# Two chunks of tokens at a time through the dense layers, with 512-column products of h

## The chip, the cores and the metric

The kernel runs on one core of one Trainium2 chip. The metric is device time in microseconds (us), the median of several executions. Engines in the rows: PE is TensorE's products, PEld its weight loads, DVE is VectorE, ACT is ScalarE, POOL is GpSimd, SP is SyncE, which issues most DMAs.

## The reference, cut to what matters

Sliding-window attention with sink tokens, then a gated two-layer block on its output:

```python
# q, k, v: (4 batches, 8 heads, 768, 64) float32; window 128, 4 sink tokens
scores = (q @ k.T) / sqrt(64)              # kept: first n_sink columns, and 0 <= row - col < window
a = exp(scores - max); a = a / (a.sum() + 1e-9)
x = (a @ v)                                # heads side by side: 3072 tokens x 512
h = x @ w_in                               # 512 x 2048, float64 in memory
g = h * cos(h)
out = g @ w_out                            # 2048 x 512, float64 in memory; out float32
```

## The kernel before, in words

The 3072 tokens are twelve chunks of 256 (`NT = CB * P`). A chunk is a batch and a first block of 128 rows. The first three chunks are the heads of batches 0 to 2 (row 0 on); then the others follow batch by batch. For each chunk eight attention heads are worked through, and their outputs become x, transposed (512 rows of 256 tokens), split into a rounded high part `xhi` and a remainder `xlo` so that a product in the reduced fp32r format keeps float32's accuracy. The weights are loaded as 64-bit words, converted on VectorE (L540 to L555), and split into `hi` and `lo` too.

The dense layers of a chunk go in eight slots (`NSLOT`) of two 128-row tiles of the hidden dimension (`FG = 2`). In a slot, `h_mm` (L411) makes h for two tiles: per tile 4 blocks of the contraction x 3 products (lo x hi, hi x hi, hi x lo), each with 128 columns of w_in as weights and 256 tokens moving. Then come, on 128 x 512 values each: `turns` (ScalarE, h in turns, rounded to a whole number), `rest` (VectorE, the remainder), `cosine` (ScalarE, sine table), `gate` (VectorE, in place in the h bank), `g_hi` (ScalarE) and `g_lo` (VectorE). `out_mm` (L467) multiplies g by w_out, 512 columns moving, and accumulates over all 16 tiles into two accumulators `acc`, one per 128 tokens. When the eight slots are done, the accumulators are copied (`out_copy`) and stored; those of the last chunk by `last_rows` (L1443), after the check whether a general path is needed. Chunk 0 takes g and w_out unsplit, in full float32 (`x.full`, L474).

PSUM has eight banks: `b0`, `b1` for the accumulators; `b4` and `b2`, and from chunk 2 on `b3` too, for h (L1418); `s` for scores, `tp` for the transposed probabilities, `av` for the attention's values product and for the sinks' transpose `gp`. A bank of h is free when `g_lo` has read it; a bank of scores when the masks have.

The order is written out by a planner, `Plan`. Each step has a priority time, an estimated duration, the engine or engines that may run it, and what it depends on: other steps, or a buffer (`buf(tag, n)`: the step waits for the users of the buffer's previous holder). `Plan.order` plays the steps through: whenever an engine is free, it takes the ready step with the smallest key, which is the priority with penalties for a change of table (`PEN`), for GpSimd or for a second-choice engine. The order so found is emitted, and each engine then runs its list in order, waiting on semaphores. The framework adds the waits, also between engines that touch one PSUM tile. The priority times are the constants `C`: slot s of chunk a stands at `S1 + ((a-1)*NSLOT + s)*T` (chunk 0 at `S0 + s*STEP`), a head at `S1 + (g - 16)*T`, so that the attention of a chunk runs one chunk ahead of its dense slots. Heads of the first 24 are computed in another way (`early`, full float32 scores, L843 to L854). ScalarE holds one table at a time: the exponentials of four heads are taken together (`softmax`, L1247), and the sine needs another table.

Beside this, 32 steps (`check_piece`, L587) load the weights once more and look for values too small for the conversion, at most one per slot from chunk 2 on. 160 products on a spare bank (`fill`, L1375) have the latest priority of all; they stand where nothing else is ready.

Of the kernel before, what the change touches and what calls it, by code (L numbers as in the profile page):

```python
# [16 lines left out]
P = 128  # L17
# [14 lines left out]
    "NWF": 0.232, "PB": 5, "PEN": 27.684, "PL": 3, "POOLF": 4.428, "POOLPEN": -1.361, "QE": 5.937, "R": 2, "RAW": 2,  # L32
# [137 lines left out]
def attn_moe_kernel(ctx, tc, q, k, v, n_sink, window, w_in, w_out, out):  # L170
# [16 lines left out]
    FG = 2  # L187
    NSLOT = NFT // FG
    WP = 2 * FG * P

    NEH = int(C["NEH"]) // 2 * 2
    NE = -(-NEH // H)
    chunks = [(b, 0) for b in range(NE)]
    chunks += [(b, i0) for b in range(B) for i0 in range(0, NB, CB) if i0 or b >= NE]
# [18 lines left out]
    yt = lp.tile([P, FG, NT], I32, name="yt")  # L213
    rc_i = yt[:, 0].rearrange("p (a c) -> p a c", a=2)
# [9 lines left out]
    tiny = cp.tile([P, NC * NSLOT // 2 + NFT], F32, name="tiny")  # L224
# [91 lines left out]
    def w_in_piece(s, c):  # L316

        rows, f0 = slice(c * P, (c + 1) * P), s * FG * P
        return Piece("in", s // 2 * NC + c, w_in[rows, 2 * f0 : 2 * (f0 + WP)] if w64 else w_in[rows, f0 : f0 + WP])

# [3 lines left out]
    w_ins = [[w_in_piece(s, c) for c in range(NC)] for s in range(0, NSLOT, 2)]  # L324
    w_outs = [w_out_piece(f) for f in range(NFT)]

    ACC = ("b0", "b1")
# [3 lines left out]
    def new_chunk():  # L331
        x = Rec()
        x.acc, x.o, x.f, x.bo = {}, {}, {}, {}
        x.sums = [[] for _ in range(NP)]
        x.parts, x.full, x.om = [], False, {}
        x.last = False
        return x

    def x_hi(x, a, p, odd):
        def fn(e):  # L340
            if p == 0 and not odd:
                x.hi = xp.tile([P, NP, NT], F32R, name=f"xhi_{a}", tag="xhi", bufs=2)
            if odd is None:
                nc.scalar.copy(out=x.hi[:, p, :], in_=x.f[p])
            else:
                r = slice(odd * 64, odd * 64 + 64)
                nc.scalar.copy(out=x.hi[r, p, :], in_=x.f[p][r, odd])
        return fn

    def x_minus(x, p):  # L350
        def fn(e):


            nc.tensor.matmul(
                out=x.f[p], lhsT=minus, rhs=x.hi[:, p, :].unsqueeze(1).broadcast_to([P, 2, NT]),
                start=False, stop=True, skip_group_check=True,
            )
        return fn

    def x_lo(x, a, p, odd):  # L360
        def fn(e):
            if p == 0 and not odd:
                x.lo = xp.tile([P, NP, NT], F32R, name=f"xlo_{a}", tag="xlo", bufs=2)
            if odd is None:
                e.tensor_tensor(out=x.lo[:, p, :], in0=x.f[p], in1=f32(x.hi)[:, p, :], op=ALU.subtract)  # L365
            else:
                r = slice(odd * 64, odd * 64 + 64)
                copy(e, x.lo[r, p, :], x.f[p][r, odd])
        return fn

    def split_x(plan, x, a, p, t, odd=None):

        add, buf = plan.add, plan.buf
        if p == 0 and not odd:
            x.bhi, x.blo = buf("xhi", 2), buf("xlo", 2)
        i = add(
            [("ACT", act(NT, odd is None))], x_hi(x, a, p, odd), x.sums[p] + (x.firsts[:1] if x.parts else [x.bhi]), t
        )
        if odd == 0:
            x.head, x.first_hi = i, x.parts == []  # L380
            if x.first_hi:
                x.firsts, x.parts = [i], [[]]
            else:
                x.parts.append([])
            return [i]
        users = [i]
        if odd is None:
            j = add(sub(NT), x_lo(x, a, p, odd), [i, x.firsts[1] if x.parts else x.blo], t + 0.3, port=True)
            if not x.parts:
                x.firsts = [i, j]  # L390
            x.parts.append([i, j])
            return users + [j]
# [3 lines left out]
        for half in range(2):  # L396
            d = [m] + x.firsts[1:2] if x.firsts[1:] else [m, x.blo]
            j = add([("ACT", act(NT, False)), ("DVE", dve(NT))], x_lo(x, a, p, half), d, t + 0.6 + 0.01 * half)
            if not x.firsts[1:]:
                x.firsts.append(j)  # L400
            users.append(j)
# [9 lines left out]
    def h_mm(o, x, t, half):  # L411
        def fn(e):
            if t == 0 and half == 0:
                o.h = env.ps.tile([P, FG, NT], F32, name=f"h_{o.m}", tag=o.bank)
            fs = slice((o.s % 2 * FG + t) * P, (o.s % 2 * FG + t + 1) * P)
            for c in range(half * NC // 2, (half + 1) * NC // 2):
                w = w_ins[o.s // 2][c]
                for n, (w, xx) in enumerate(((w.lo, x.hi), (w.hi, x.hi), (w.hi, x.lo))):
                    nc.tensor.matmul(  # L419
                        out=o.h[:, t, :], lhsT=w[:, fs], rhs=xx[:, c, :],  # L420
# [10 lines left out]
    def rest(o):  # L431
        def fn(e):
            o.r = mp.tile([P, FG, NT], F32, name=f"r_{o.m}", tag="r", bufs=C["R"])
# [15 lines left out]
    def gate_full(o):  # L449
        def fn(e):  # L450
            o.g32 = mp.tile([P, FG, NT], F32, name=f"g_{o.m}", tag="ghi", bufs=C["GHI"])
            nc.vector.tensor_tensor(out=o.g32, in0=o.h, in1=o.r, op=ALU.mult)
        return fn

    def g_hi(o):
        def fn(e):
            o.ghi = mp.tile([P, FG, NT], F32R, name=f"ghi_{o.m}", tag="ghi", bufs=C["GHI"])
# [3 lines left out]
    def g_lo(o):  # L461
        def fn(e):
            o.glo = mp.tile([P, FG, NT], F32R, name=f"glo_{o.m}", tag="glo", bufs=C["GLO"])
# [3 lines left out]
    def out_mm(o, x, t, j):  # L467
        def fn(e):
            f = o.s * FG + t
            if f == 0:  # L470
                x.acc[j] = (env.pa if x.banks is ACC else env.ps).tile([P, DM], F32, name=f"acc_{o.m}_{j}", tag=x.banks[j])
            w = w_outs[f]
            if x.full:
                nc.tensor.matmul(  # L474
                    out=x.acc[j], lhsT=o.g32[:, t, j * P : (j + 1) * P], rhs=w.w32, start=(f == 0), stop=(f == NFT - 1)
                )
                return
            for n, (gg, w) in enumerate(((o.ghi, w.hi), (o.ghi, w.lo), (o.glo, w.hi))):
                nc.tensor.matmul(  # L479
                    out=x.acc[j], lhsT=gg[:, t, j * P : (j + 1) * P], rhs=w,  # L480
                    start=(f == 0 and n == 0), stop=(f == NFT - 1 and n == 2), skip_group_check=x.last,
                )
        return fn

    def out_end(o, x, j, half):
        def fn(e):
            cs = slice(half * DM // 2, (half + 1) * DM // 2)
            for t in range(FG):
                f = o.s * FG + t
                w = w_outs[f]  # L490
                for n, (gg, w) in enumerate(((o.ghi, w.hi), (o.ghi, w.lo), (o.glo, w.hi))):
                    nc.tensor.matmul(
                        out=x.acc[j][:, cs], lhsT=gg[:, t, j * P : (j + 1) * P], rhs=w[:, cs],
                        start=False, stop=(f == NFT - 1 and n == 2), skip_group_check=True,
# [9 lines left out]
    def out_store(x, a, j):  # L504
        def fn(e):
            b, i0 = chunks[a]
            r0 = b * S + (i0 + j) * P
# [97 lines left out]
    def dense(plan, x, a, s, t, T, w_in_ready, w_out_ready, acc_banks, h_bank):  # L605

        add, buf = plan.add, plan.buf
        if s == 0:
            x.bacc = [buf(b, 1) for b in acc_banks]
            x.banks = acc_banks  # L610
            if not x.parts:
                x.bhi, x.blo, x.parts = Buf(None), Buf(None), [[]] * NP
        accs = x.bacc
        if True:
            o = Rec()
            o.s, o.m, o.bank = s, a * NSLOT + s, h_bank
            bh, by, br, bhi, blo = buf(h_bank, 1), buf("y", 1), buf("r", C["R"]), buf("ghi", C["GHI"]), None if x.full else buf("glo", C["GLO"])
            mm = []
            for tt in range(FG):
                for half in range(2):  # L620
                    d = x.parts[2 * half] + x.parts[2 * half + 1] + w_in_ready[s]
                    d += mm[:1] if mm else [bh]
                    mm.append(
                        add([("PE", 0.655)], h_mm(o, x, tt, half), d + mm[-1:], t + C["DH"] + (3.5, 5.8)[tt] + 0.6 * half)
                    )
            x.bhi.users += mm
            x.blo.users += mm
            a0 = add([("ACT", act(FG * NT, False))], turns(o), mm + [by], t + C["DM"] + 7.2)
            a2 = add([("DVE", dve(FG * NT))], rest(o), [a0, br], t + C["DM"] + 8.0)
            by.users.append(a2)  # L630
# [974 lines left out]
```

## Time and profile before

| What | us |
|---|---|
| Median of 3 runs (739.83 to 743.51) | 743.26 |
| Profiled execution, span from the first to the last instruction | 740.6 |
| TensorE busy | 723.9 (98%) |
| VectorE busy | 628.0 (85%) |
| ScalarE busy | 557.2 (75%) |
| GpSimd busy | 106.4 (14%) |
| 16 DMA engines, mean share, queue of SP | 39.2% |

The page gives no total of the profiled execution beside its span. Products are pipelined: a 256-column product shows 0.28 us of busy time, but the next starts 0.12 us later, so what a product costs is read from the starts or from the chain, and a busy TensorE may still have small gaps. Idle time of an engine that is not on the chain costs nothing. The granted TensorE clock is 1.00 from 18 us on to the end of the products.

### The profile page before, as it was taken

To read this page: it belongs to the slowest core of one execution; us is meant where nothing else is said; L and a number is where in the kernel's file an instruction comes from. 1 tells how busy PE (TensorE), PEld (TensorE's weight loads), DVE (VectorE), ACT (ScalarE), POOL (GpSimd) and SP (SyncE) were. 2 spreads that over 40 slices of the span, in tenths; PEclk is the share of its full clock that TensorE was granted. 3 is DMA by queue.
4 is the path that set the end of the run, shared out by engine and by line. 5 is a ranking of instruction groups with operands and counts; after the bars stand their busy time and mean duration, and the time that the engine had idled before them with its cause. 6 is when DMAs were issued, how large, how long until landed. Compare 5 with 4: busy or idle time off the path is not lost.

```text
span 740.6 us, 15107 instructions
## 1 busy us (share of the span) xinstructions
PE 723.9 (98%) x4827; PEld 644.6 (87%) x4827; DVE 628.0 (85%) x1778; ACT 557.2 (75%) x1387; POOL 106.4 (14%) x191
## 2 busy tenths in 40 slices
PE   9989999999999999999999999999999999999996
PEld 8777776799899998998999889999998999999995
DVE  6999999777899999999999999897989888965432
ACT  4889969566978878799787898788888698884322
POOL 1000000001121221222212122122001122212000
PEclk9999999999999999999999999999999999999999
DMA  5765565232455455465466443232342232110000
GB/s 155 196 180 183 158 187 162 56 49 39 105 143 122 109 137 141 96 169 127 104 157 163 92 105 54 54 67 43 54 87 49 47 77 51 35 39 8 30 1 32
DMA packets 215896, 71.48 MB, mean 97 GB/s; under 512 B 204288, under 2 KB 204800, under 8 KB 215808
## 3 DMA queue, kind: packets, MB, share of 16 engines
q1 hardware_dynamic: 215232, 70.17, 39.2%
q8 instruction: 40, 0.66, 0.4%
q14 instruction: 48, 0.39, 0.2%
q10 hardware_dynamic: 576, 0.26, 0.1%
HBM read 64.10 MB, written 6.29 MB: 95 GB/s over the span
## 4 chain that ended last, share of the span: by engine, by line
PE 79%; DVE 9%; ACT 7%; DMA 3%; issue 1%; SPq 1%; DVEq 0%; ACTq 0%
PE h L419 32%; PE acc L479 31%; PE av L1101 5%; PE s L906 5%; PE tp L1021 2%; ACT p L951 1%; ACT p L928 1%; DVE p L919 1%; DMA xk<-in_k_dram 1%; DMA raw<-in_moe_w_in_dram 1%; PE acc L474 1%; DMA xq<-in_q_dram 1%; DVE lo_in L582 1%; PE av L1077 1%; DVE w_out L546 1%
## 5 line engine op out<-in xcount | busy, mean ns | idle before, releaser
L419 PE MATMUL h<-xhi,lo_in 128*128 128x256 f32 x768 | 226.0, 294 | 2.9 <-ACT firsts L407 1.6
L419 PE MATMUL h<-xlo,hi_in 128*128 128x256 f32 x768 | 217.0, 283 | 0.4 <-DVE xlo L365 0.4
L419 PE MATMUL h<-xhi,hi_in 128*128 128x256 f32 x768 | 216.7, 282 | 0.0
L419 PEld LDWEIGHTS h<-xhi,lo_in 128*128 128x128 f32 x768 | 146.0, 190 | 8.1 <-ACT firsts L407 1.8
L419 PEld LDWEIGHTS h<-xhi,hi_in 128*128 128x128 f32 x768 | 146.3, 191 | 3.2 <-issue 1.1
L419 PEld LDWEIGHTS h<-xlo,hi_in 128*128 128x128 f32 x768 | 146.1, 190 | 0.6 <-DVE xlo L365 0.6
L479 PE MATMUL acc<-hi_out,ghi 128*128 128x512 f32 x350 | 142.3, 406 | 0.2 <-ACT raw L407 0.2
L479 PE MATMUL acc<-lo_out,ghi 128*128 128x512 f32 x350 | 137.4, 393 | 0.0
L479 PE MATMUL acc<-hi_out,glo 128*128 128x512 f32 x350 | 137.4, 393 | 0.0
L1060 POOL TENSOR_SCALAR_AFFINE_SELECT pz<-pz 128x512 fp32r<-128x512 f32 x128 | 83.4, 652 | 285.4 <-DVE pz L1047 212.5
L919 DVE CUSTOM_DVE_ANT_0 p<-s,mk 128x264 f32<-128x264 f32 (+1 forms) x192 | 75.5, 400 | 24.6 <-PE s L906 20.1
L428 ACT ACTIVATE yt<-h 128x512 int32<-128x512 f32 x96 | 57.2, 596 | 49.9 <-PE h L419 49.4
L928 ACT ACTIVATE p<-p,st 128x264 f32<-128x264 f32 (+1 forms) x192 | 93.6, 491 | 0.6
L434 DVE SCALAR_TENSOR_TENSOR r<-h,yt 128x512 f32<-128x512 f32 x96 | 65.5, 682 | 26.0 <-ACT yt L428 25.8
L441 ACT ACTIVATE r<-r,neg 128x512 f32<-128x512 f32 x96 | 69.3, 724 | 13.9 <-DVE r L434 13.0
L479 PEld LDWEIGHTS acc<-hi_out,glo 128*128 128x128 f32 x350 | 65.8, 188 | 14.9
L479 PEld LDWEIGHTS acc<-hi_out,ghi 128*128 128x128 f32 x350 | 65.9, 188 | 8.6 <-ACT raw L407 0.6
L479 PEld LDWEIGHTS acc<-lo_out,ghi 128*128 128x128 f32 x350 | 66.1, 189 | 7.6
L464 DVE TENSOR_TENSOR glo<-h,ghi 128x512 fp32r<-128x512 f32 x88 | 60.0, 682 | 11.5 <-ACT ghi L458 10.8
L446 DVE TENSOR_TENSOR h<-h,r 128x512 f32<-128x512 f32 x88 | 60.3, 687 | 8.2 <-ACT r L441 8.0
L458 ACT CAST ghi<-h 128x512 fp32r<-128x512 f32 x88 | 51.3, 583 | 16.1 <-PE acc L479 12.9
L906 PE MATMUL s<-r,l 128*128 128x264 f32 (+2 forms) x288 | 59.6, 288 | 0.8 <-DVE st L919 0.7
(140 smaller groups left out, 1286.2 us busy)
## 6 DMA issues: line engine op xcount, KB each, us to landing
raw<-in_moe_w_in_dram SPq DMA_DIRECT2D x32, 512.0 KB
raw<-in_moe_w_out_dram SPq DMA_DIRECT2D x32, 512.0 KB
xk<-in_k_dram SPq DMA_DIRECT2D x256, 48.0 KB
v<-in_v_dram SPq DMA_DIRECT2D x64, 96.0 KB
out_dram<-raw SPq DMA_DIRECT2D x22, 256.0 KB
xq<-in_q_dram SPq DMA_DIRECT2D x144, 32.0 KB
v<-in_v_dram SPq DMA_DIRECT2D x32, 64.0 KB
xq<-in_q_dram SPq DMA_DIRECT2D x24, 64.0 KB
```

Of the source, the lines that this page charges most:

```text
L419: nc.tensor.matmul(out=o.h[:, t, :], lhsT=w[:, fs], rhs=xx[:, c, :], start=(c == 0 and n == 0), stop=(c == NC - 1 and n == 2),)
L428: nc.scalar.activation(out=yt, in_=o.h, func=AF.Copy, scale=INV2PI, bias=0.25)
L434: nc.vector.scalar_tensor_tensor(out=o.r, in0=o.h, scalar=INV2PI, in1=yt, op0=ALU.mult, op1=ALU.subtract)
L441: nc.scalar.activation(out=o.r, in_=o.r, func=AF.Sin, scale=TWOPI_DOWN, bias=quarter)
L446: nc.vector.tensor_tensor(out=o.h, in0=o.h, in1=o.r, op=ALU.mult)
L458: nc.scalar.copy(out=o.ghi, in_=o.h)
L464: e.tensor_tensor(out=o.glo, in0=o.h, in1=f32(o.ghi), op=ALU.subtract)
L479: nc.tensor.matmul(out=x.acc[j], lhsT=gg[:, t, j * P : (j + 1) * P], rhs=w, start=(f == 0 and n == 0), stop=(f == NFT - 1 and n == 2), ski ...
L906: nc.tensor.matmul(out=o.s_ps[j][:, :w], lhsT=o.l[:, j * P : (j + 1) * P], rhs=r.rearrange("p n s -> p (n s)")[:, c0 : c0 + w], start=(n = ...
L919: nc.vector.tensor_tensor_reduce(out=o.p[:, j, :w], in0=o.s_ps[j][:, :w], in1=masks[min(o.i0 + j, 2)][:, :w], op0=ALU.add, op1=ALU.min, sc ...
L928: nc.scalar.activation(out=o.p[:, j, :w], in_=o.p[:, j, :w], func=AF.Exp, bias=o.lead.st[:, 0, o.nth, j : j + 1], scale=-1.0, accum_out=o. ...
L1060: nc.gpsimd.affine_select(out=env.pz4[:, :, :, n], in_=f32(env.pz4)[:, :, :, 0], pattern=[[0, 2], [0, CB], [sign, P]], compare_op=ALU.is_g ...
```

## The change

From chunk 2 on, two chunks go through the dense layers together. There are seven units: chunk 0 and chunk 1 alone, then five pairs. The chunk order is changed so that all four (b, 0) chunks come first; the first 24 heads are the same. x of both chunks of a pair lies in one tile, `[P, NP, UC, NT]`, so that 512 tokens are one moving operand. A slot of a pair is one hidden tile x 512 tokens (16 slots a pair) where it was two tiles x 256 tokens (8 slots a chunk); the tile of h and the gate steps keep their 512 values. A pair has four accumulators.

The banks: accumulators `b0` to `b3`, h in `h0` and `h1` throughout, `s`, and `tp`. For heads past the first row block, `tp`, `av` and `gp` are halves of that one bank (`half_bank`); the first-row heads use `tp` whole and `b2` (or `h1`) for av. The planner holds the halves as two buffers.

The last pair has no attention beside it. `last_rows` copies four accumulators instead of two, and the products of the last two slots are put in order of accumulator (`JL`). Checks begin with unit 2. Almost all constants of `C` have new values. The compiler's scratch for dynamic DMAs is set to 256.

```diff
-    "S0": -10.291, "S1": 61.51, ... "STEP": 7.406, "T": 7.838, ... "LAG": 4.632, ... "PEN": 27.684,
+    "S0": -9.306, "S1": 60.82, ... "STEP": 7.945, "T": 9.553, ... "LAG": 7.555, ... "PEN": 15.951, "JL": 14.55,
...
+    UC = 2
+    NU = UC * NT
+    NJ = UC * CB
+    WF = 4
...
+    chunks = [(b, 0) for b in range(B)] + [(b, i0) for b in range(B) for i0 in range(CB, NB, CB)]
+    pairs = [[n, n + 1] for n in range(0, len(chunks), UC)]
+    units = [[n] for n in pairs[0]] + pairs[1:]
...
-    ACC = ("b0", "b1")
+    ACC = tuple(f"b{j}" for j in range(NJ))
...
+        x.fg = UC // x.nk
+        x.nslot = NFT // x.fg
+        x.nj = x.nk * CB
...
                     nc.tensor.matmul(
-                        out=o.h[:, t, :], lhsT=w[:, fs], rhs=xx[:, c, :],
+                        out=o.h[:, t * w_n : (t + 1) * w_n], lhsT=w[:, fs],
+                        rhs=xx[:, c, ks].rearrange("p k n -> p (k n)"),
...
+                d = parts[2 * half] + parts[2 * half + 1] + w_in_ready[f] + (mm[:1] or [bh]) + mm[-1:]
...
+        def half_bank(n):
+            if not hasattr(env, "tpav"):
+                env.tpav = bank("tp", [P, 2, NT], "tpav")
+            return env.tpav[:, n]
...
-                o.tp = ps.tile([P, 4 * P], F32, name=f"tp_{o.tag}", tag=o.tp_bank)
+                o.tp = half_bank(0) if o.one else bank(o.tp_bank, [P, 4 * P], f"tp_{o.tag}")
...
-                o.av = ps.tile([P, NT], F32, name=f"av_{o.tag}", tag="av")
+                o.av = half_bank(1) if o.one else bank(o.av_bank, [P, NT], f"av_{o.tag}")
...
-            return C["E"][a] + h * C["TE"][a] if a < NE else C["S1"] + (g - (NE - 1) * H) * T
+            return C["E"][a] + h * C["TE"][a] if a < NE else C["S1"] + (g - NE * H) * T
...
-            return C["S1"] + ((a - 1) * NSLOT + s) * T if a else C["S0"] + s * C["STEP"]
+            return C["S1"] + (sum(x.nslot for x in xs[1:a]) + s) * T if a else C["S0"] + s * C["STEP"]
...
-            hs = ("b4", "b2") if a < NE - 1 else ("b4", "b2", "b3")
+            parts = [sum((xc[n].parts[p] for n in units[a]), []) for p in range(NP)]
+            acc_banks = ACC[: xs[a].nj] if xs[a].nk == 1 else ACC[2:] + ACC[:2]
...
+                ("h0", "h1")[nh % 2],
```

## Rows read from the trace of the kernel before

**Rows 1.** The page, part 1: busy us (share of the span), instructions of each engine.
```profile
PE 723.9 (98%) x4827; PEld 644.6 (87%) x4827; DVE 628.0 (85%) x1778; ACT 557.2 (75%) x1387; POOL 106.4 (14%) x191
```
**Rows 2.** The page, part 4: the chain that ended last, by engine.
```profile
PE 79%; DVE 9%; ACT 7%; DMA 3%; issue 1%; SPq 1%; DVEq 0%; ACTq 0%
```
**Rows 3.** Waits of PE, first and last of 14: us in total, times, longest.
```profile
PE h L419 <- ACT firsts L407: 1.6, 1, 1.6
...
PE acc L479 <- ACT raw L407: 0.2, 1, 0.2
```
**Rows 4.** Groups by line: form xcount | busy us, mean ns | idle before, releasers.
```profile
L419 PE MATMUL h<-xhi,lo_in 128*128 128x256 f32 x768 | 226.0, 294 | 2.9 <-ACT firsts L407 1.6 <-DVE glo L464 1.0 <-DVE g L452 0.3
...
L479 PE MATMUL acc<-hi_out,ghi 128*128 128x512 f32 x350 | 142.3, 406 | 0.2 <-ACT raw L407 0.2
...
L434 DVE SCALAR_TENSOR_TENSOR r<-h,yt 128x512 f32<-128x512 f32 x96 | 65.5, 682 | 26.0 <-ACT yt L428 25.8
L446 DVE TENSOR_TENSOR h<-h,r 128x512 f32<-128x512 f32 x88 | 60.3, 687 | 8.2 <-ACT r L441 8.0
L464 DVE TENSOR_TENSOR glo<-h,ghi 128x512 fp32r<-128x512 f32 x88 | 60.0, 682 | 11.5 <-ACT ghi L458 10.8
...
L928 ACT ACT_TABLE_LOAD x21 | 26.9, 1283 | 0.4
...
L595 DVE CUSTOM_DVE_ANT_0 raw<-raw 128x512 f32<-128x512 f32 x32 | 21.7, 679 | 0.8 <-DMA raw<-in_moe_w_in_dram 0.8
...
L953 DVE TENSOR_SCALAR p<-p,st 128x136 f32<-128x136 f32 (+2 forms) x61 | 15.5, 307 | 0.1
```
**Rows 5.** The chain in order of time, near its end: start us, us, what.
```profile
697.86 5.75 PE h L419 x48
703.61 4.79 PE acc L479 x21
...
722.51 10.23 PE acc L479 x45
```
**Rows 6.** Windows: length, busy us (xcount) of PE, PEld, DVE, ACT, POOL; clock, DMA.
```profile
350.00:400.00 50.00, 49.84 (x353) 45.92 (x353) 47.89 (x137) 39.00 (x94) 10.91 (x20) 1.00 0.55 136
20.00:640.00 620.00, 611.41 (x4104) 542.65 (x4103) 566.85 (x1625) 502.29 (x1262) 93.68 (x163) 1.00 0.44 106
0.00:20.00 20.00, 18.33 (x116) 16.66 (x117) 13.08 (x52) 9.68 (x31) 2.87 (x11) 1.00 0.60 164
0.00:130.00 130.00, 122.58 (x712) 95.77 (x712) 117.40 (x324) 102.13 (x272) 3.24 (x12) 1.00 0.61 174
60.00:120.00 60.00, 58.28 (x309) 41.97 (x307) 57.31 (x141) 50.08 (x126) 0.00 (x0) 1.00 0.63 179
120.00:172.00 52.00, 51.54 (x310) 42.80 (x309) 42.11 (x94) 34.68 (x78) 1.45 (x5) 1.00 0.28 65
172.00:232.00 60.00, 59.80 (x419) 54.86 (x417) 52.86 (x158) 46.16 (x115) 11.88 (x20) 1.00 0.48 117
0.00:679.00 679.00, 668.74 (x4485) 594.94 (x4486) 607.62 (x1745) 539.24 (x1356) 105.14 (x189) 1.00 0.43 104
```
**Rows 7.** Timeline of DVE at 262 us: start us, us, what.
```profile
261.84 0.65 DVE L464 TENSOR_TENSOR glo<-h,ghi 128x512 fp32r<-128x512 f32 x1
```
**Rows 8.** Timeline of PE at 263 us.
```profile
263.27 0.28 PE L419 MATMUL h<-xhi,lo_in 128*128 128x256 f32 x1
```
**Rows 9.** Timeline of ACT from 250 to 262 us, its table loads.
```profile
251.20 1.28 ACT L928 ACT_TABLE_LOAD   x1
...
261.66 1.28 ACT L441 ACT_TABLE_LOAD   x1
```
**Rows 10.** Timeline of PE at 269 us: transposes of one head.
```profile
268.94 0.38 PE L1021 MATMUL tp<-ident,p 128*128 128x128 f32 x2
```
**Rows 11.** Timeline of ACT at 269 us: the copy of the sinks' transpose.
```profile
268.89 0.37 ACT L407 CAST gt<-gp 64x256 fp32r<-64x256 f32 x1 [1.66 <-PE gp L1005]
```
**Rows 12.** Timeline of DVE at 684 us: the last part of x.
```profile
683.66 0.43 DVE L365 TENSOR_TENSOR xlo<-x,xhi 128x256 fp32r<-128x256 f32 x1 [0.47 <-ACT xhi L344]
```

More of the change, by code (lines that the diff above doesn't have):

```diff
@@ L337, in new_chunk, with x_tile, x_hi @@
-        return x
-    def x_hi(x, a, p, odd):
+        x.parts = [[] for _ in range(NP)]
+        return x
+    def x_tile(what, name):
+        return xp.tile([P, NP, UC, NT], F32R, name=name, tag=what, bufs=2)
+    def x_hi(x, a, p, odd, new):
         def fn(e):
-            if p == 0 and not odd:
-                x.hi = xp.tile([P, NP, NT], F32R, name=f"xhi_{a}", tag="xhi", bufs=2)
+            if new:
+                x.u.hi = x_tile("xhi", f"xhi_{a}")
             if odd is None:
-                nc.scalar.copy(out=x.hi[:, p, :], in_=x.f[p])
+                nc.scalar.copy(out=x.u.hi[:, p, x.k], in_=x.f[p])
@@ L396, in split_x @@
         for half in range(2):
[L397 to L400, printed above, removed]
+            new = not u.firsts[1:]
+            d = [m, *(u.firsts[1:2] or [u.blo])]
+            j = add(
+                [("ACT", act(NT, False)), ("DVE", dve(NT))], x_lo(x, a, p, half, new), d, t + 0.6 + 0.01 * half
+            )
+            if new:
+                u.firsts.append(j)
             users.append(j)
@@ L472, in fn @@
             w = w_outs[f]
+            js = slice(t * x.nk * NT + j * P, t * x.nk * NT + (j + 1) * P)
             if x.full:
                 nc.tensor.matmul(
-                    out=x.acc[j], lhsT=o.g32[:, t, j * P : (j + 1) * P], rhs=w.w32, start=(f == 0), stop=(f == NFT - 1)
+                    out=x.acc[j], lhsT=o.g32[:, js], rhs=w.w32, start=(f == 0), stop=(f == NFT - 1)
                 )
                 return
[L478 to L491, printed above, removed]
+            for half in range(halves):
+                cs = slice(half * DM // halves, (half + 1) * DM // halves)
+                for n, (gg, ww) in enumerate(((o.ghi, w.hi), (o.ghi, w.lo), (o.glo, w.hi))):
@@ L492, in fn @@
                     nc.tensor.matmul(
-                        out=x.acc[j][:, cs], lhsT=gg[:, t, j * P : (j + 1) * P], rhs=w[:, cs],
-                        start=False, stop=(f == NFT - 1 and n == 2), skip_group_check=True,
+                        out=x.acc[j][:, cs], lhsT=gg[:, js], rhs=ww[:, cs],
+                        start=(f == 0 and n == 0), stop=(f == NFT - 1 and n == 2), skip_group_check=x.last,
                     )
@@ L655, in dense @@
-        if s < NSLOT - 1 or (x.last and a == len(chunks) - 1):
+        o = Rec()
+        o.s, o.m, o.bank = s, a * NFT + s, h_bank
+        fs = range(s * x.fg, (s + 1) * x.fg)
+        bh, by, br, bhi, blo = buf(h_bank, 1), buf("y", 1), buf("r", C["R"]), buf("ghi", C["GHI"]), None if x.full else buf("glo", C["GLO"])
+        mm = []
+        for tt, f in enumerate(fs):
+            for half in range(2):
+                d = parts[2 * half] + parts[2 * half + 1] + w_in_ready[f] + (mm[:1] or [bh]) + mm[-1:]
+                mm.append(add(
+                    [("PE", 0.655 * x.nk + 0.05 * (x.nk - 1))], h_mm(o, x, tt, half), d,
+                    t + C["DH"] + 3.5 + 2.3 * tt + 0.6 * x.nk * half,
+                ))
@@ new lines, in dense @@
+        x.pair.bhi.users += mm
+        x.pair.blo.users += mm
+        a0 = add([("ACT", act(NU, False))], turns(o), mm + [by], t + C["DM"] + 7.2)
+        a2 = add([("DVE", dve(NU))], rest(o), [a0, br], t + C["DM"] + 8.0)
+        by.users.append(a2)
+        a3 = add([("ACT", act(NU) + 0.09)], cosine(o), [a2], t + C["DM"] + 8.9, table="sin")
+        if x.full:
+            a4 = add([("DVE", dve(NU))], gate_full(o), [a3, bhi], t + C["DM"] + 9.5)
+            br.users.append(a4)
+            bh.users += [a0, a2, a4]
+            gs = [a4]
+        else:
+            a4 = add([("DVE", dve(NU))], gate(o), [a3], t + C["DM"] + 9.5)
+            br.users.append(a4)
+            a5 = add([("ACT", act(NU, False))], g_hi(o), [a4, bhi], t + C["DM"] + 10.2)
+            a6 = add([("DVE", dve(NU))], g_lo(o), [a5, blo], t + C["DM"] + 10.8)
+            bh.users += [a0, a2, a4, a5, a6]
+            gs = [a5, a6]
@@ new lines, in dense @@
+        for tt, f in enumerate(fs):
+            for j in range(x.nj):
+                d = gs + w_out_ready[f] + (accs[j].users[: None if f == NFT - 1 else 1] or [accs[j]])
+                late = C["JL"] * j if x.last and s >= x.nslot - 2 else 1.95 * tt + (0.3, 0.65)[x.nk - 1] * j
+                mm = out_mm(o, x, tt, j, 2 if x.last and f == NFT - 1 and j == x.nj - 1 else 1)
+                i = add([("PE", 0.858 if x.full else 0.655)], mm, d, t + C["LAG"] * T + late)
+                bhi.users.append(i)
+                if not x.full:
+                    blo.users.append(i)
+                x.om.setdefault(f, []).append(i)
+                accs[j].users.append(i)
@@ L656, in dense @@
+        if s < x.nslot - 1 or x.last:
             return
-        for j in range(CB):
+        for j in range(x.nj):
             bo = x.bo[j] = buf("raw", C["RAW"])
@@ L1431, in banded_path @@
         if w64:
-            t = slots[8 + 2 * NSLOT + len(checks)][0]
-            btp = buf("tp", 1)
+            t = slots[min(sum(x.nslot for x in xs[: C["CU"]]) + len(checks) + 8, len(slots) - 4)][0]
+            btp = half_buf(0)
             i = add([("DVE", 0.16)], least_all, checked, t)
@@ L1570, in attn_moe_kernel @@
         with ExitStack() as ctx2:
-            general_path()
+            general_path(x.acc)
     with rare.Else():
```

261 lines of the change are left out of this document (120 added, 141 removed), and 13 rows, old and new, of the table C.

## The prediction

> **What bounds the kernel now.** I read the page's busy shares first: TensorE 723.9 of 740.6 us, VectorE 628.0, ScalarE 557.2 [rows 1]. The reader is to see two engines that are nearly full, not one. The chain that ended last gives TensorE 79% and no other engine more than 9% [rows 2]. TensorE's waits confirm it: 14 kinds, the longest 1.6 us in all, the shortest 0.2 [rows 3]. So the end is set by the sum of TensorE's products, and a product made cheaper shows in the time unless TensorE then has to wait.
>
> Next the groups by line, for what is issued: 3 x 768 products of h with 256 columns and 3 x 350 products of acc with 512 columns [rows 4]. Their busy times overlap, so what one costs is read from the chain in order of time, where nothing else lies between: 48 h products take 5.75 us, 119.8 ns each; 21 acc products 4.79 us, 228.1 ns, and 45 of them 10.23 us, 227.3 ns [rows 5]. Twice the columns cost 1.90 to 1.91 times as much, so some 11 to 12 ns of each product is not columns.
>
> Last the stretches, for the second engine. VectorE is busy 47.89 of 50 us at 350 to 400, 566.85 of 620 at 20 to 640 (91.4%), but only 42.11 of 52 at 120 to 172 [rows 6]. It is where a gain on TensorE can be lost.
>
> **The change part by part.** The profile has a span and no total of its own; the median of the runs is 743.26 us, so 2.7 us is taken as lying around the span, before and after. The sum is made on the span.
>
> *Products of h.* Chunks 0 and 1 stay single (2 x 192 products of 256 columns). The other ten go as five pairs: 5 x 16 x 4 x 3 = 960 products of 512 columns instead of 1920 of 256. If a 512-column h product costs what an acc product costs, one pair saves 2 x 119.8 - 228.1 = 11.5 ns [rows 5], 960 of them 11.0 us (11.8 by the 45-product row). TensorE is the chain here, so all of it counts. No 512-column product with x as its moving operand is in this trace, so the other end is no saving; I take -11.0, the operand type and column count being those of the acc rows.
>
> The Trainium skill (TensorE: Matmul & The Clock Gate, section Back-to-back issue gap) speaks against that size: it gives N/2.4 + 2.5 ns per warm product, so merging two would save only 2.5 ns, 2.4 us in all by an estimate from its formula. Its 109 ns for 256 columns is below the 119.8 here, so the trace disagrees; it comes back as a rival.
>
> *Everything else that is issued.* Acc products, gate operations (one turn, rest, sine, gate and split per 512 values, 96 times before and after), attention heads and weight conversion keep their counts. The order of chunks changes: chunk 3 is (3,0), eight heads without lap and sink work, now early; a little cheaper where it lands, as much dearer later. Twice the x tiles cost SBUF only.
>
> *Two h banks instead of three.* From chunk 2 on h had b4, b2, b3; now h0, h1 all through. The third bank is in use: the split that frees a bank begins at 261.84 and takes 0.65 us, and the next h begins at 263.27 [rows 7, 8]. Behind a late h stand, in TensorE's queue, everything planned after it: attention products and acc. The cover now is a third slot's h (24 products, 2.88 us by rows 5) while ScalarE sits in a batch of exponentials: the table goes to exp at 251.20 and back to sine at 261.66, 10.5 us in which no sine runs [rows 9]. There are 18 such batches (72 heads by fours). Bounds: 0, if the split of the two waiting slots is placed ahead of each batch; 18 x 2.88 = 52 us if each loses all the cover. The nearest row is the stretch 120 to 172, dense work with two h banks, TensorE 51.54 of 52 [rows 6]; I take +1.5.
>
> *Transposes and values in one bank.* For heads with i0 > 0, tp and av become two halves of one bank, and gp too. Today they are apart, and they do meet: the transposes of one head start at 268.94 and last 0.38 us, while ScalarE reads gp from 268.89 on for 0.37 [rows 10, 11]; 7 of the 64 such heads come within 0.2 us of a read of av or gp. The Trainium skill (PSUM — Partial Sum Buffer, section PSUM bank collisions raise a hardware error) says two engines on one bank and the same quadrant must be kept apart in time, disjoint columns or not; no run here shows it. Whatever the order puts between them, the price of a meeting is about that 0.37 us: 7 x 0.37 = 2.6 us at today's order, 64 x 0.37 = 24 if every head meets, 0 if none does. I take +0.5.
>
> *First hand-over.* Unit 2 now needs chunks 2 and 3, so the eight heads of chunk 3 must be through before its first h; before, they ran beside chunk 2's dense slots. At 172 to 232 VectorE was busy 52.86 us: nine slots at 0.682 + 0.687 + 0.682 = 18.5, five checks at 0.76 (3.8), so about 30 for these heads [rows 4, 6]. Ahead of 172 it has 60 - 57.31 and 52 - 42.11 = 12.6 us free; ScalarE has 27 [rows 6]. What doesn't fit is up to 18 us of waiting; what hides it is ScalarE taking copies and normalising, and the checks, which need not run yet. Bounds 0 and +18, taken +1.
>
> *Last pair.* Attention must be done before sixteen pure dense slots instead of eight. The last x part is at 683.66 now [rows 12], 57 us before the end. A pure slot is 2.88 + 12 x 0.228 = 5.6 us, of 512 columns 5.5, so eight more put the last x part about 100 us before the end, at 634 of a span of 734. VectorE's work until then: 607.6 by 679, some 3 more, less 16.4 for eight slots that are now behind it, about 594; less the first 20 us (13.1), 581 in 614: 94.6% [rows 6]. That is above today's 91.4 and below the best 50 us (95.8). Moving 15.5 us of normalising to ScalarE [rows 4] would bring it to 92%. Bounds: 0; or, at today's 91.4%, 581/0.914 = 636 instead of 614, +22. Taken +2.
>
> *Tail and queues.* Four accumulators are copied out at the end instead of two, but three are finished while products of the others run; the last one's copy and store are the old ones: 0. Stores and loads on SP keep their number, with checks moved some slots earlier in the order; 0, since the longest of TensorE's waits is 1.6 us in all whatever it names [rows 3].
>
> Sum: -11.0 + 1.5 + 0.5 + 1 + 2 = -6.0: span 734.6, time 737.3 us.
>
> **The rivals.**
> 1. *VectorE paces the attention and the last pair starts late* (slower). Place: the stretch 20 to 634; it decides from where VectorE can't hold 94.6%. At 91.4% the span is 734.6 - 2 + 22 = 754.6, time 757; halfway 747. For it: VectorE is already the second engine, and waits are made of queue order. Against it: 95.8% was held at 350 to 400 with TensorE at 49.84 of 50 [rows 6], and ScalarE has room.
> 2. *Two h banks run dry in each batch of exponentials.* At a quarter of the lost cover, 18 x 0.7 = 13 us instead of 1.5: 749. For it: rows 7 to 9; against it: rows 6 at 120 to 172, without attention.
> 3. *The wider product saves nothing*: an h product's time is by its columns, 512 of them cost 2 x 119.8 ns, -11.0 becomes 0, time 748. For it: a row of an h product with 512 columns is missing. Against it: the acc rows [rows 5]. By the Trainium skill's formula (same page and section) the saving would be 2.4 us and the time, as an estimate, 746.
> 4. *The new order also closes gaps.* TensorE is idle 130 - 122.58 = 7.4 us in the first 130 us [rows 6], where loads and conversion pace it. With that, and none of the losses: 743.3 - 11 - 4 = 728.
>
> **How the numbers follow.** Forecast 0.50 (730 to 744), rival 1 0.17, rival 2 0.12, rival 3 0.06, rival 4 0.15. The bound of 0.5% is 3.7 us: faster is below 739.5, slower above 747. The forecast gives 0.38 faster and 0.11 same, rival 4 0.15 faster, rivals 1 to 3 together 0.11 same and 0.24 slower: with a hundredth of the forecast's 0.50 slower, 0.53, 0.22 and 0.25. Range 726 to 752: it takes in rival 4, rival 2 and the lower half of rival 1, and leaves out VectorE at today's share.
>
> **What would show it.** Right: h products of 512 columns in the chain at 228 ns a step, 960 fewer TensorE instructions, TensorE's busy share still 97 to 98%, VectorE about 95% until the last x part at about 634. Wrong: a step near 239 ns (rival 3); TensorE waiting for glo or the sine's result each 28 us (rival 2), for xlo ahead of the last pair or at the first hand-over (rival 1), or for the sums of av before a transpose.

## The result, and the profile after

The changed kernel takes 752.5 us (median of 4 runs, 751.61 to 753.72), the kernel before 741.96 beside it: 1.0137 times, 95% interval 1.0118 to 1.0156. It is slower by 10 us where 6 us of gain were forecast, and just above the range. The profiled spans are 749.9 and 740.6 us at the same granted clock, 0.998. The chain of waits of the changed kernel breaks off after six pieces, so what follows is read from counts, stretches and waits.

The page, part 1 [rows 1]: 963 instructions fewer on TensorE, at the same busy share; GpSimd has 94 more and VectorE 74 fewer.
```profile
PE 725.5 (97%) x3864; PEld 589.7 (79%) x3864; DVE 617.9 (82%) x1704; ACT 555.7 (74%) x1369; POOL 177.7 (24%) x285
```
Groups by line, shapes apart [rows 4]; idle time before them behind the second bar:
```profile
L510 PE MATMUL acc<-hi_out,ghi 128*128 128x512 f32 x351 | 141.4, 403 | 0.0
...
L446 PE MATMUL h<-xhi,lo_in 128*128 128x512 f32 x320 | 128.5, 402 | 2.0 <-DVE glo L492 1.6
...
L462 DVE SCALAR_TENSOR_TENSOR r<-h,yt 128x512 f32<-128x512 f32 x96 | 65.5, 683 | 52.6 <-ACT yt L456 52.3
```
An h product of 512 columns is as long as one of acc. VectorE waits 52.3 us for ScalarE's turns where it waited 25.8 [rows 4].

Stretches, columns as in [rows 6]:
```profile
20.00:640.00 620.00, 602.92 (x3283) 487.86 (x3284) 563.23 (x1583) 507.17 (x1270) 172.63 (x271) 1.00 0.45 106
0.00:130.00 130.00, 123.88 (x728) 97.22 (x729) 116.15 (x333) 107.50 (x286) 7.37 (x18) 1.00 0.63 168
130.00:640.00 510.00, 497.08 (x2666) 406.14 (x2665) 460.53 (x1305) 410.77 (x1019) 168.13 (x264) 1.00 0.42 93
651.00:730.00 79.00, 79.00 (x350) 65.44 (x349) 29.71 (x45) 26.49 (x44) 0.00 (x0) 1.00 0.04 14
```
Ahead of 130 us nothing is lost (123.88 busy, 122.58 before). From 651 us on, where only dense work is left, 350 products of 512 columns fill 79.00 us, 225.7 ns each. The loss is between: from 130 to 640 us TensorE is idle 12.9 of 510 us. The same stretch of the kernel before, 2.8 us idle:
```profile
130.00:640.00 510.00, 507.16 (x3507) 463.54 (x3507) 462.53 (x1353) 409.84 (x1021) 93.30 (x162) 1.00 0.41 91
```
The waits of TensorE are now of 20 kinds instead of 14 [rows 3], and none is large. First and last of them:
```profile
PE h L446 <- DVE glo L492: 2.1, 5, 0.6
...
PE tp L1047 <- ACT p L973: 0.2, 1, 0.2
```

A matmul's end is modelled, so busy time hides short waits. I therefore also add up, in each trace, the time from each product's start to the next one's: the median of its kind (line, tiles, shape) is counted as product time, what goes beyond it as waiting. The median step of an h product is 227 ns at 512 columns; at 256 it is the 119.8 of [rows 5].

| kernel | time, us | product time | waiting to 130 us | 130 to 640 us |
|---|---|---|---|---|
| before | 742.0 | 712.8 | 12.0 | 8.0 |
| after | 752.5 | 700.1 | 10.2 | 33.0 |
| e1_order: chunk order | 755.9 | 715.1 | 12.7 | 19.5 |
| e2_two_h: e1, two h banks | 771.2 | 714.9 | 13.0 | 28.2 |
| e3_share: e1, shared bank | 760.8 | 715.1 | 13.5 | 22.1 |
| e4_both | 775.3 | 714.9 | 12.7 | 31.8 |
| e5_split: after, 256 columns | 760.6 | 713.8 | 12.4 | 25.5 |
| e6_small: after, short checks | 749.4 | 699.8 | 11.4 | 28.9 |
| e10_ownav_same: after, av apart | 747.9 | 699.2 | 10.8 | 28.9 |
| e13_after_refit | 754.4 | 701.1 | 13.2 | 31.2 |
| e14_before_refit | 746.9 | 713.5 | 16.7 | 6.9 |
| e15_both_refit | 754.8 | 715.5 | 13.0 | 16.7 |
| e16_order_refit | 741.1 | 713.5 | 12.9 | 6.2 |
| e17_share_fitted | 743.6 | 713.6 | 11.9 | 8.0 |
| e18_two_h_refit | 754.4 | 713.3 | 24.2 | 8.3 |

The change takes 12.7 us of product time away and adds 23 of waiting: 25 more between 130 and 640 us, 1.8 less ahead of it. Two things limit what one row can tell. Up to 188 us the change, e5 and e6 run the same instructions, and their waiting to 130 us is 10.2, 12.4 and 11.4; so differences of some 2 us are no more than one trace can tell. And in e1 to e4, e10, e13, e14 and e18 the granted clock falls to 0.50 for a while, which counts as waiting here; in the other kernels of the table it is 1.00 from 7 us on until the products end.

The loss is not even. The stretch up to the first h product of a pair, at 188.7 us in the change (the first h of chunk 2 starts at 172.6 us before), in the kernel before, in e15 (the structure of the change without pairs), in e5 and in the change:
```profile
130.00:190.00 60.00, 60.00 (x390) 53.05 (x390) 46.89 (x118) 36.61 (x84) 4.37 (x11) 1.00 0.23 46
```
```profile
130.00:190.00 60.00, 60.00 (x391) 53.07 (x390) 44.54 (x116) 37.78 (x84) 0.31 (x1) 1.00 0.21 42
```
```profile
130.00:190.00 60.00, 57.52 (x355) 47.15 (x354) 56.56 (x145) 52.31 (x136) 15.26 (x21) 1.00 0.39 81
```
```profile
130.00:190.00 60.00, 56.94 (x352) 46.73 (x351) 55.78 (x145) 51.57 (x131) 15.45 (x22) 1.00 0.39 80
```
With pairs TensorE is idle 2.5 to 3.1 of these 60 us, without them not at all, and VectorE is busy 56 us instead of 45 to 47. Counted from start to start it waits there 4.5 us in e5 and 5.3 in the change, and 0.2 or less in the other two; e13, the change with constants chosen anew, waits 3.5 there. This is the first hand-over: the heads of two chunks have to be through before it instead of those of one.

### The profile page after: what moved, and what is told of

The parts are those of the page before. It is cut to its first block, busy times and chain, and to the rows that moved or that the text cites. A ratio compares the mean times of both kernels' runs of the same rounds, so it can differ in the third digit from the quotient of the medians.

```text
span 749.9 us, 13236 instructions
## 1 busy us (share of the span) xinstructions
PE 725.5 (97%) x3864; PEld 589.7 (79%) x3864; DVE 617.9 (82%) x1704; ACT 555.7 (74%) x1369; POOL 177.7 (24%) x285
## 5 line engine op out<-in xcount | busy, mean ns | idle before, releaser
L446 PE MATMUL h<-xhi,lo_in 128*128 128x512 f32 (+1 forms) x448 | 167.9, 375 | 2.5 <-DVE glo L492 2.1
L446 PE MATMUL h<-xlo,hi_in 128*128 128x512 f32 (+1 forms) x448 | 161.5, 360 | 0.0
L446 PE MATMUL h<-xhi,hi_in 128*128 128x512 f32 (+1 forms) x448 | 161.0, 359 | 0.0
L1082 POOL TENSOR_SCALAR_AFFINE_SELECT pz<-pz 128x512 fp32r<-128x512 f32 x128 | 85.9, 671 | 135.5 <-DVE pz L1069 109.6
L462 DVE SCALAR_TENSOR_TENSOR r<-h,yt 128x512 f32<-128x512 f32 x96 | 65.5, 683 | 52.6 <-ACT yt L456 52.3
L446 PEld LDWEIGHTS h<-xhi,lo_in 128*128 128x128 f32 x448 | 84.4, 188 | 20.2 <-DVE glo L492 7.5
L446 PEld LDWEIGHTS h<-xlo,hi_in 128*128 128x128 f32 x448 | 84.4, 188 | 13.2
L446 PEld LDWEIGHTS h<-xhi,hi_in 128*128 128x128 f32 x448 | 84.6, 189 | 11.4 <-issue 0.2
L928 PE MATMUL s<-r,l 128*128 128x264 f32 (+2 forms) x288 | 63.7, 300 | 2.8 <-DVE r L919 1.7
L988 POOL TENSOR_TENSOR vr<-v,vr 128x192 fp32r<-128x192 f32 (+1 forms) x54 | 35.1, 650 | 119.0 <-ACT vr L983 119.0
L928 PEld LDWEIGHTS s<-r,l 128*128 128x128 f32 x288 | 49.2, 189 | 17.0 <-DVE st L941 6.0
```

The source lines that it names most:

```text
L446: nc.tensor.matmul(out=o.h[:, t * w_n : (t + 1) * w_n], lhsT=w[:, fs], rhs=xx[:, c, ks].rearrange("p k n -> p (k n)"), start=(c == 0 and n ...
L462: nc.vector.scalar_tensor_tensor(out=o.r, in0=o.h, scalar=INV2PI, in1=yt, op0=ALU.mult, op1=ALU.subtract)
L928: nc.tensor.matmul(out=o.s_ps[j][:, :w], lhsT=o.l[:, j * P : (j + 1) * P], rhs=r.rearrange("p n s -> p (n s)")[:, c0 : c0 + w], start=(n = ...
L988: e.tensor_tensor(out=o.vr[:, :, 1, :], in0=o.v32, in1=f32(o.vr)[:, :, 0, :], op=ALU.subtract)
L1082: nc.gpsimd.affine_select(out=env.pz4[:, :, :, n], in_=f32(env.pz4)[:, :, :, 0], pattern=[[0, 2], [0, CB], [sign, P]], compare_op=ALU.is_g ...
```

## The experiments

**One part at a time, on the kernel before.** e1 has only the new order of chunks, with the constants of the order left as they were; e2 and e3 add one part each, e4 both.
```diff
-    chunks = [(b, 0) for b in range(NE)]
-    chunks += [(b, i0) for b in range(B) for i0 in range(0, NB, CB) if i0 or b >= NE]
+    chunks = [(b, 0) for b in range(B)] + [(b, i0) for b in range(B) for i0 in range(CB, NB, CB)]   # e1 to e4
-                hs = ("b4", "b2") if a < NE - 1 else ("b4", "b2", "b3")
+                hs = ("b4", "b2")                                                                # e2, e4
-                o.av = ps.tile([P, NT], F32, name=f"av_{o.tag}", tag="av")
+                o.av = half_bank(1) if o.one else ps.tile(...)       # e3, e4; tp is half_bank(0), gp half_bank(1)
```


> The kernel before with only the order of chunks changed: (3,0) is chunk 3. Base for the next three. If the banks are the cause (theory B) or the load on VectorE and the early hand-over of pairs (theory V): both expect 742 +- 2 us, since no bank goes and nothing must be ready earlier. More than 745 would put part of the loss on the order itself.

> e1 with two h banks throughout, the third left empty; single chunks, constants of before. Theory B, h part: the loss of the third bank makes TensorE wait for the split of h, 5 to 10 us over e1. Theory V: TensorE finds attention and acc products instead, at most 2 us over e1.

> e1 with transposes and values of the later heads in halves of one bank, three h banks. Theory B, shared part: waits between engines that the planner doesn't hold, 5 to 10 us over e1, seen as TensorE waiting before transposes and values. Theory V: at most 2 us over e1.

> e1 with both: two h banks and the shared bank, but single chunks with 256-column products. Theory B: 752.5 + 12 us that the wide products save, so 760 to 766, the whole loss without the pairs. Theory V: 742 to 748, the loss comes with the pairs.

The theories that the expectations name: V, VectorE's load and the early hand-over of pairs; B, the banks; O, further down, the order itself.

Measured: e1 1.0178 times before [1.0154, 1.0201], which neither theory expected; e2 1.0394 [1.0361, 1.0427]; e3 1.0248 [1.0218, 1.0278]; e4 1.044 [1.0412, 1.0468]. The order of chunks alone, with constants that were chosen for another order, costs 14 us, so the 15 us of the two h banks and the 5 of the shared bank above it may be the banks' or the constants'. Under these constants the two parts add up: 15.3 + 4.9 us against 19.4 for both. Hence the second half of the experiments.

**One part at a time, on the kernel after.** e5 computes each 512-column h product as two of 256 in the same order. e6 lets the 32 checks of the weights read 16 of 512 columns (that part of the check is left out), e12 does the same to the kernel before.
```diff
-                    nc.tensor.matmul(out=o.h[:, t * w_n : (t + 1) * w_n], ..., rhs=xx[:, c, ks]...)
+                    for k in range(x.nk):                                                        # e5
+                        nc.tensor.matmul(out=o.h[:, t * w_n + k * NT :][:, :NT], ..., rhs=xx[:, c, x.k0 + k], ...)
-                out=top, in0=top, in1=top, op0=ALU.mult, op1=ALU.max, ...
+                out=top[:, :16], in0=top[:, :16], in1=top[:, :16], op0=ALU.mult, op1=ALU.max, ... # e6, e12
```


> The changed kernel in its own order and banks, but every 512-column product of h of a pair issued as two of 256 columns (960 more products). If TensorE's own time is what counts, 960 x 11.5 ns come back: 752.5 + 11 = 763.5 us. If TensorE waits for others anyway (theory V: VectorE paces), the products fill waits: 753 to 757. By products of 2.5 ns fixed cost alone: 755.

> The changed kernel in its own order, with the 32 checks reading 16 columns instead of 512 (most of the check is left out): VectorE is relieved of about 17 us between unit 2 and the middle, nothing else changes. Theory V (VectorE's load paces): 742 to 747 us. Theory B (banks, and waits in the given order): 749 to 752, the waits for a bank are shortened only where a check stands in the way.

> The kernel before in its own order, with the checks reading 16 columns (most of the check is left out): the counterpart of e6. If the relief of VectorE counts for as much here, 739 us (-3); if the changed kernel is nearer to VectorE's limit than the one before, 741 to 742 (0 to -1).

e5: 1.0235 [1.0216, 1.0255], 8.1 us above the change. The width saves 13.7 us of product time, and 7.5 come back as waiting between 130 and 640 us (25.5 to 33.0); ahead of 130, where the two run the same instructions, the change happens to wait 2.2 us less, which makes 8.4 for the 8.1 measured. The reading, argued and not shown wait by wait, is that the slower products had covered for work that now comes late. e6: 1.0097 [1.008, 1.0114], 3.1 us below the change; e12: 1.0 [0.9987, 1.0012]. In e6 VectorE's check takes 266 ns instead of 743 [rows 4 have 679]:
```profile
L613 DVE CUSTOM_DVE_ANT_0 raw<-raw 128x16 f32<-128x16 f32 x32 | 8.5, 266 | 5.1 <-DMA raw<-in_moe_w_out_dram 2.5 <-DMA raw<-in_moe_w_in_dram 2.4
```
So 15 us less of VectorE's work give the changed kernel 3 and the old one nothing: VectorE delays TensorE at places, its total doesn't pace it. The checks begin with unit 2, so e6 takes nothing from VectorE in the first hand-over, and doesn't test whether VectorE paces that.

**The banks given back, on the kernel after.** A pair has four accumulators; one bank is freed by adding two of them into the same bank, which leaves their separate sums out. e7 and e8 put the order together anew with the same constants, e9 to e11 keep the change's order of instructions.
```diff
-  ("h0", "h1")[nh % 2]
+  ("h0", "h1", "b3")[nh % 3]                                                  # e7; e9, e11: same order
-  o.av = half_bank(1) if o.one else bank(o.av_bank, [P, NT], f"av_{o.tag}")
+  o.av = bank("b3" if o.one else o.av_bank, [P, NT], f"av_{o.tag}")           # e8; e10, e11: same order
```


> The changed kernel with a third h bank, its order planned with it. The bank is got by letting the fourth accumulator of a pair write into the third's bank, so two rows of blocks of the output are left out; the work issued is the same. Theory B: 738 to 744 us, the fifteen us that two banks cost with the constants of before come back for the most part. Theory V: 750 to 753.

> As the last, but the freed bank is given to av and gp of the later heads, so that transposes and values no longer share one; two h banks. Theory B, shared part: 746 to 749 us (5 us with the constants of before). Theory V: 750 to 753.

> The changed kernel with every engine's list in the order it has now, but h of the pairs rotating over three banks instead of two, so that only the semaphore waits for a bank get shorter. The bank is got by letting accumulator 1 of a pair write into accumulator 0's bank (those rows of the output are left out). Theory B: the waits of h for the split of two slots before go, 752.5 - 6 = 746 to 749 us. Theory O (the order itself is late everywhere: each engine's list was fitted to durations that it doesn't keep, whatever the banks): 751 to 753.

> As the last, with two h banks, and the freed bank for av and gp of the later heads: only the waits that come of sharing a bank go, the order stays. Theory B, shared part: 746 to 749 us. Theory O: 751 to 753.

> Both in the same order: own bank for av and gp, and three h banks from the second pair on (accumulators 1 and 3 of a pair are merged into 0 and 2). Theory B: 741 to 745 us, that is, the loss over the kernel before is the banks. Theory O: 750 to 753.

e7 1.0263 [1.0245, 1.0282] and e8 1.0176 [1.0143, 1.0209], both slower than the change: again an order with constants not chosen for it. e9 1.0165 [1.0133, 1.0197], 2.3 us slower: counted from start to start, TensorE's waits for glo fell from 4.1 to 1.0 us, but those for st, the statistics of the scores, rose from 3.9 to 6.7. e10 1.0085 [1.0058, 1.0111], 4.6 us faster. Both carry the merged accumulator too: TensorE waits 1.2 us in e9 and 0.9 in e10 for copies of it (ACT raw), in the change not at all. e11 1.0289 [1.0261, 1.0316] settles nothing, since the merged accumulators make TensorE wait 9.4 us for their copies.

What e10 takes away can be seen. Timeline of the change at 301 us, start us, us, what, idle time before: ScalarE copies P out of one half of the bank, and VectorE's sum of x, in the other half, begins 0.03 us after the end of it.
```profile
301.05 0.37 ACT L1060 CAST pz<-tpav 128x256 fp32r<-128x256 f32 x1
...
301.45 0.42 DVE L1137 TENSOR_TENSOR x<-tpav,xb 64x256 f32<-64x256 f32 x1 [0.23 <-ACT pz L1060]
```
The same two in the kernel before, from two banks, overlap:
```profile
308.48 0.37 ACT L1038 CAST pz<-tp 128x256 fp32r<-128x256 f32 x1
308.53 0.42 DVE L1115 TENSOR_TENSOR x<-av,xb 64x256 f32<-64x256 f32 x1
```
Of the 72 copies 38 overlap a sum of x in the kernel before, 4 in the change (all four of heads that have banks of their own), 42 in e10; 40 in e1 and 1 in e3. The waits of VectorE and ScalarE that stand for it in the change (us in total, times, longest):
```profile
DVE x L1137 <- ACT pz L1060: 7.5, 19, 1.2
```
```profile
ACT pz L1060 <- DVE x L1137: 3.8, 11, 0.5
```
The Trainium skill (PSUM — Partial Sum Buffer, section PSUM bank collisions raise a hardware error) asks for such accesses to be kept apart; here they are, by the program's waits. What the chip does without them no run shows.

**Constants chosen again.** To separate banks from constants, the written-out order was replayed engine by engine, with each kind's step from the two traces, and the constants of the order searched for the shortest end of the replay, in the same way for five kernels. Only the table C differs, for example:
```diff
-    "LAG": 4.632, "POOLF": 4.428, "POOLPEN": -1.361, "S1": 61.51,
+    "LAG": 4.14, "POOLF": 4.753, "POOLPEN": 12.728, "S1": 66.619,      # e16, 38 constants in all
```


> The changed kernel with its structure untouched (pairs, two h banks, shared bank), only the constants of the order chosen again, for the shortest end of a replay: the written-out order run engine by engine with each kind's step from the two traces, 0.07 us from engine to engine, and the accesses to the shared bank one after the other. The replay ends at 724.0 us for the change as made (span measured 749.9, so 25.9 are not in it) and at 712.7 for this one. Theory O (the loss is the fit of the order): span 712.7 + 25.9 = 738.6, time 741, 736 to 746. Theory B (the loss is in the banks themselves, whatever the order): 748 to 755.

> Control: the kernel before with its constants chosen again by the same search. Replay 724.2 us as made (span measured 740.6, 16.4 not in it), 708.9 now. If the replay can be trusted across orders: span 725.3, time 728. If a search on the replay only trades what it sees against what it doesn't see (what the replay leaves out grows to the 26 us of the changed orders): 708.9 + 25.9 = 734.8, time 737.5. If the order shown was fitted on something better than this replay: 742 or more, and then e13 says little about how good an order the changed structure can have.

> The kernel before with new order of chunks, two h banks and shared bank (e4_both, 775 us), with constants chosen again by the same search: the structure of the change without its wide products. Replay 743.1 as e4_both (773 measured), 721.1 now. Theory O: 721 + 30 = 751, time 754, which is some 13 above e13 (the wide products' worth). Theory B: 765 or more.

> The kernel before with the new order of chunks alone (e1_order, 756 us), constants chosen again by the same search. Replay 729.8 as e1_order (755.6 measured), 713.7 now. Theory O: 713.7 + 25.8 = 739.5, time 742, so that the order of chunks costs nothing by itself. Rival: the order of chunks itself costs: 750 or more.

Measured: e13 1.0145 [1.0123, 1.0168], e14 1.0061 [1.0045, 1.0078], e15 1.0154 [1.0135, 1.0174], e16 0.9981 [0.9971, 0.9991]. The order of chunks costs nothing once its constants fit it: e16 is 15 us faster than e1. The control e14 loses 4.6 us, all of it ahead of 130 us (16.7 instead of 12.0 us of waiting; why the replay misses that stretch is not shown); behind 130 us it waits 6.9 us against 8.0, so there the search is as good as the order shown. The changed structure stays at 754 with it, against theory O's 736 to 746. By the expectation of e14, at 742 or more e13 says little about how good an order the changed structure can have; that the search holds its own behind 130 us is all that speaks for it. And e15 and e13 take the same time although e13 has 14.4 us less product time: its waiting is 14.5 us more.

**The two banks apart, in fitted orders.** e17 is e16 with the edit of e3 and nine constants moved a little, so that every engine keeps the order of e16; e18 is e16 with the edit of e2 and constants chosen again.

> e16_order_refit (741.1 us) with the transposes and the values of a head in two halves of one bank, in exactly the order of e16. Replay 713.7 to 718.8. Theory B: the shared bank costs in a fitted order what it cost in the others or more, 4.6 to 8: 746 to 749; VectorE's sums of x wait for ScalarE's copies of P some 20 to 30 times, and these two no longer overlap. Theory O (a fitted order hides it): 741 to 743.

> e16_order_refit (741.1 us) with two h banks instead of three all through, own banks for transposes and values, constants chosen again by the search. Replay 714.8, against 713.7 of e16 and 740.7 with e16's constants. Theory O (two banks are enough once the order fits them): 742 to 744, so that of e15's 13.6 us nearly all is the shared bank or the two together. Theory B (two banks cost by themselves): 748 or more.

e17 1.0017 [1.0004, 1.003], 2.5 us above e16; e18 1.0139 [1.0109, 1.0169], 13 us above. By its time alone e18 would make the two h banks the cause, as theory B had it. Its stretches say otherwise (columns as in [rows 6]):
```profile
0.00:130.00 130.00, 114.43 (x650) 89.71 (x651) 109.84 (x301) 91.78 (x242) 21.57 (x29) 0.97 0.55 157
130.00:640.00 510.00, 508.03 (x3472) 459.99 (x3472) 444.23 (x1216) 394.99 (x966) 193.59 (x308) 1.00 0.42 95
```
e16 for comparison, and e15:
```profile
0.00:130.00 130.00, 120.85 (x699) 94.41 (x700) 113.21 (x313) 98.83 (x263) 5.49 (x17) 1.00 0.61 171
130.00:640.00 510.00, 507.57 (x3510) 463.82 (x3509) 467.09 (x1360) 409.22 (x1015) 93.10 (x165) 1.00 0.42 92
```
```profile
130.00:640.00 510.00, 501.51 (x3433) 453.39 (x3432) 460.52 (x1340) 402.06 (x985) 88.14 (x159) 1.00 0.41 92
```
With two h banks TensorE is idle 2.0 of the 510 us from 130 on, no more than in e16; of e18's 13 us 11.3 lie ahead of 130, where TensorE is idle 15.6 us instead of 9.2, GpSimd has 21.57 us of work instead of 5.49 (the constant that weighs its time fell from 4.8 to 0.7) and the mean clock is 0.97. The bank can't be the cause there: the third h bank is in use from chunk 2 on, whose first h starts at 173.6 us in e16 and 188.8 in e18. It is the search's constants. With both banks taken (e15) the idle time from 130 on is 8.5 us.

## Why the prediction was wrong

**What held.** TensorE sets the end and the wide product costs what an acc product costs: 227 ns forecast as 228; product time fell by 12.7 us for a forecast of 11.0. Rival 3 is refuted, in both its forms (nothing saved, or 2.4 us). The order of chunks costs nothing (e16). Two h banks alone, in an order chosen for them, cost 2.1 us of waiting from 130 us on (8.3 against 6.2) for a forecast of 1.5; rival 2's 13 us are not there, though its sign, waits for glo, shows in part (1.6 us before, 4.1 in the change). The shared bank alone costs 2.5 us in a fitted order and 4.6 to 4.9 in the others, for a forecast of 0.5 with a bound of 24. The price of a meeting was right in kind, a copy of 0.37 us, but not who meets: the prediction counted TensorE's transposes against reads of av (7 heads), and what had to be kept apart was ScalarE's copy and VectorE's sum, which overlapped 38 times before and wait for each other some 30 times now. Ahead of 130 us nothing is lost, and little ahead of the last pair (TensorE is busy 51.62 of the 52 us from 600 on). The last part of x came at 647 us, 103 us before the end where about 100 were forecast; 13 us later than the forecast 634, since the kernel was late by then.

Rival 1's outcome came: VectorE at 90.8% (563.23 of 620) and not 95, a late last pair, a time within 747 to 757. Its cause is refuted for the stretch behind 190 us, since taking 15 us from VectorE gives 3 (e6), and no wait for xlo ahead of the last pair shows. For the first hand-over it is open.

**What failed.** Three terms, and the adding up.

1. "TensorE is the chain here, so all of it counts": of 13.7 us of product time that the width saves, 7.5 come back as waiting between 130 and 640 us in the same order (e5 against the change).
2. The first hand-over, taken at +1 of 18: it costs 4.5 to 5.3 us of waiting by 190 us, in e5 and in the change, and nothing without pairs.
3. The banks, 1.5 + 0.5: in e15, which has both and no pairs, TensorE waits 10.5 us more than in e16.

The sum took its parts as small and as independent of each other, 1.5 + 0.5 + 1 + 2 = 5 us, and measured were 25 between 130 and 640 us. In waiting there, step by step: order of chunks -1.8 (before to e16), two h banks +2.1 (e18), shared bank +1.8 (e17), both together +6.6 beyond the two (e15: 16.7 - 6.2 - 2.1 - 1.8), pairs +8.8 (e5 25.5 - e15 16.7), some 5 of them in the first hand-over, width +7.5 (after 33.0 - e5). They add up to 25.0; each comes from one trace of either kernel, and is good to some 2 us at best.

Which waits grew fits this: many, and none of them large. Counted from start to start, for glo from 1.6 to 4.1 us, and for GpSimd's and VectorE's pz, r, p and gc, each below 1 us before, 2.0 to 3.0 now; for what a late product waited is inferred. The prediction read rows 3, no wait above 1.6 us in all, as a sign that only the products count; an order without reserve looks the same.

**What stays open.** That the two banks take from one slack, so that both cost more than the sum, is argued: the 6.6 us stand between orders that were each searched for once, while with the constants left as they were (e1 to e4) the two parts just add. The pairs' 8.8 us are between two kernels whose constants come from different searches; what holds TensorE up in the first hand-over, VectorE at 93% or the order of the heads, and what the rest is, was not taken apart. The change's constants also give GpSimd 71 us more work; as a load that costs nothing in e18, which has 193.59 us of it from 130 on and waits 8.3, but TensorE's waits for GpSimd's pz are among those that grew. Nor is it shown that no order does better: e13's search found none from 130 us on (31.2 against 33.0). A kernel with e18's order behind 130 us and e16's ahead of it was not run; neither has wide products.

No kernel here beats the one before by more than e16's 0.2%, and e16 is the order of chunks alone.

## What to carry to other kernels

Where one engine is at 98% by a written-out order, a resource taken from that order (a bank, a buffer, the length of a covering product, a unit that must be complete earlier) is not priced by its own row alone: here the parts were forecast at 5 us, with nothing for the lost cover, and came to 25. Constants of an order are part of the kernel: changing the structure below them and not them cost 14 us in e1, and nothing with constants chosen anew (e16), so an ablation needs its constants chosen again, and a control that shows what the choosing itself is worth. And a total says little about where an experiment lost its time: 11 of e18's 13 us were ahead of the stretch that it was to test, and some 5 of the pairs' 9 us ahead of the first product of a pair.

## What the runs showed of the hardware

Two h products of 256 columns take 2 x 119.8 = 239.6 ns and one of 512 takes 227: some 12 ns of a product are not columns, for h as for acc. An idle stretch of TensorE can cost more than its length. In e1 TensorE is idle 1.9 of the 5 us from 470 on; in the next 5 us the granted clock is 0.50, the lower of its two levels, 1.2 GHz, and it is back at the upper one, 2.4 GHz, from about 482 on:
```profile
470.00:475.00 5.00, 3.06 (x17) 1.92 (x15) 4.83 (x20) 4.90 (x12) 0.48 (x1) 0.99 0.41 66
475.00:480.00 5.00, 4.42 (x20) 4.12 (x21) 2.71 (x11) 2.07 (x6) 1.27 (x2) 0.50 0.24 48
...
485.00:490.00 5.00, 5.00 (x40) 4.73 (x39) 4.70 (x13) 3.04 (x7) 1.43 (x3) 1.00 0.10 23
```
20 products run in the second stretch, 40 in the last. In e18 such falls come three times ahead of 132 us (the mean clock is 0.66 at 76 to 81, 110 to 115 and 127 to 132 us).
